# Attention scores: from half-array pairs to full-array matmuls with stacked keys

## The chip, the cores and the metric

The kernel runs on one core of a Trainium2 chip. The metric is the device time of one execution in microseconds: 1443.77 us, the median of three runs (1442.9 to 1447.32).

## The reference

Multi-head attention with two mixes over the heads, followed by two MLPs. Inputs are q, k, v of shape (4, 12, 448, 64); the rest is

```
scores = 1/sqrt(64) * q @ k^T                       # per head
scores = einsum('bhij,hg->bgij', scores, w_pre)     # mix over the 12 heads
attn   = softmax(scores)
attn   = einsum('bhij,hg->bgij', attn, w_post)
x      = (attn @ v)  as 1792 tokens x 768
x      = (s * relu(x @ w_in)**2 + b) @ w_out        # 768 -> 2048 -> 768
h      = x @ w_in2;  out = (h * cos(h)) @ w_out2
```

All of it is float32. The kernel splits the operands of the scores, the first mix and the MLPs into a high part of type float32r and the rest, and adds up three products, high x high, high x rest and rest x high; the mix after the softmax and the product with v are plain float32.

## The kernel before

The attention works on 16 blocks, four per batch, of 120, 110, 110 and 110 query rows. Per block and pair of heads (six groups g), `scores` makes two tiles of rows x 448 in PSUM, ScalarE or VectorE copies each to SBUF (L362, L364), and a DMA on SP's queue stores it into the block's tile m, in which the partition is row and head together (10 rows x 12 heads = 120 partitions): these are the DMAs `m<-s`, or `m<-at` for block 0. Then follow 12 or 11 tiles of 120 x 448 per block, 180 in all. Each is split (L417 or L419 high part, L422 rest), mixed on TensorE (L427 to L429, three passes against a 120 x 120 weight), its maximum taken (L438, VectorE), exponentiated (L445, ScalarE), and mixed a second time with the transposing matmul L467, whose weight w (L458) carries the reciprocal of the sums. `vps` (L502) multiplies with v and `x<-xo` stores the result. The MLPs follow (L747, L810, L838); their first steps overlap the last tiles.

The operands of a score come as follows. `keys(b, g, p)` loads two heads with two DMAs into the two 64-wide halves of a raw tile, so that four transposes (L289) give a PSUM tile whose partitions 0 to 63 are one head and 64 to 127 the other. One ScalarE instruction writes the high part of both heads (L294), one VectorE instruction the rest (L296). `queries(n, g, p)` does the same for six heads of a block with one DMA: three transposes (L318), two evictions (L323, L325), two groups per block. `prod` in `scores` then makes six matmuls with K = 64: with `tile_position=(64 * z, 0)` the two heads of a group use the two halves of the array's rows side by side, three times, for the three products.

The order of the work on every engine is written by a planner (`Plan`). Each step has a position `pos`, a cost and what it waits for; `run` plays the program with these costs, gives an engine that comes free the step of lowest position among those that are ready, and emits the instructions in that order. The engines then work through their queues in order. Buffers are rings: a step that takes a buffer is not placed before the one that used it last. `STEP` is the distance of two tiles' positions, `LEAD` the position of the first tile, `OFF` says how many steps ahead of a tile's second mix its parts are due, `W1` and `W2` say where between the tiles of the block before the scores of odd and of other blocks lie, `W3` the same of keys, `PRO` the positions of block 0. All DMAs are issued by SP, in order.

Of the kernel before, what the change touches and what calls it, by code (L numbers as in the profile page):

```python
# [10 lines left out]
F32 = mybir.dt.float32  # L11
F32R = mybir.dt.float32r
I32 = mybir.dt.int32
U32 = mybir.dt.uint32
AF = mybir.ActivationFunctionType
ALU = mybir.AluOpType
# [169 lines left out]
    return c  # L186


STEP = 2484.5
LEAD = 15618.0  # L190


def attention(pl, tc, q, k, v, w_pre, w_post, cst, x, mid, left, right, psl, psr):

    nc = tc.nc
    B, H, S, D = q.shape
# [12 lines left out]
    k_p = pool(right, "a_k", side="right")  # L209
# [11 lines left out]
    def dma(pos, out, in_, nbytes, after=(), take=(), use=(), behind=()):  # L221
        return pl.add(pos, "sp", 515.0 if not use else 700.0, lambda: nc.sync.dma_start(out=out(), in_=in_()), after, take, use, nbytes=nbytes, behind=behind)
# [36 lines left out]
    kh, k_done = {}, {}  # L259
# [10 lines left out]
    def keys(b, g, p):  # L270
        hk = kh[b, g] = pl.hold(f"k{g}")
        hr = scratch[0] if b == 0 else pl.hold("rk")
        raw = lambda: piece(0, g * KW, KW)[:CH].rearrange("p (z w) -> p z w", w=2 * D) if b == 0 else hr.tile

        def load(h):
            if b and h == 0:
                hr.tile = rk_p.tile([CH, 4, 2 * D], F32, tag="rk", name="rk")
            return raw()[:, :, h * D:(h + 1) * D]
        d = []
        for h in range(2):  # L280
            d.append(dma(p - 6000, lambda h=h: load(h), lambda h=h: k[b, 2 * g + h].rearrange("(p z) d -> p z d", z=4), CH * KW * 2,
                         take=[hr] if b and h == 0 else [], behind=d if h else m_done[0][-1:] if b else [s_open]))
        bank, ring, tag = (ps_s, "ps", "s") if b else (ps_a, "pa", "a") if g % 2 else (ps_p, "pp", "p")
        hp = pl.hold(ring)

        def trans():
            hp.tile = bank.tile([128, 512], F32, tag=tag, name="tk")[:, :S]
            for z in range(4):
                nc.tensor.transpose(hp.tile[:, z * CH:(z + 1) * CH], raw()[:, z], ident[:CH, :CH])  # L289
        a = pl.add(p, "pe", 440.0, trans, d + [d_id], take=[hp, hk], use=[hr])  # L290

        def hi():
            hk.tile = k_p.tile([128, 2, S], F32R, tag=f"ks{g}", name="ks")
            nc.scalar.activation(out=hk.tile[:, 0], in_=hp.tile, func=AF.Copy)  # L294
        a = pl.add(p + 500, "act", 430.0, hi, [a])
        k_done[b, g] = [pl.add(p + 1000, "dve", 540.0, lambda: nc.vector.tensor_tensor(  # L296
            out=hk.tile[:, 1], in0=hp.tile, in1=hk.tile[:, 0].bitcast(F32), op=ALU.subtract), [a], use=[hp])]


    qh, q_done = {}, {}  # L300
# [1 line left out]
    def queries(n, g, p):  # L302
        b, (i0, rows) = n // 4, BLOCKS[n % 4]
        hr, hp = pl.hold("rq") if n else scratch[0], pl.hold("ps")
        hq = qh[n, g] = pl.hold("q")
        raw = lambda: (hr.tile if n else piece(0, 6 * KW + g * 6 * D, 6 * D))[:rows].rearrange("p (z d) -> p z d", d=2 * D)

        def load():
            if n:
                hr.tile = rq_p.tile([128, 6 * D], F32, tag="rq", name="qn")  # L310
            return raw().rearrange("p z (a d) -> p (z a) d", d=D)
        d = dma(p - 8000 if n else p - 5500, load, lambda: q[b, 6 * g:6 * g + 6, i0:i0 + rows, :].rearrange("h i d -> i h d"), rows * 3072,
                take=[hr] if n else [], behind=m_done[0][5:6] if n else [s_open])

        def trans():
            hp.tile = ps_s.tile([128, 512], F32, tag="s", name="tq")[:, :3 * rows].rearrange("p (z w) -> p z w", z=3)
            for z in range(3):
                nc.tensor.transpose(hp.tile[:, z], raw()[:, z], ident[:rows, :rows])  # L318
        a = pl.add(p, "pe", 3 * rows * .87, trans, [d, d_id], take=[hp, hq], use=[hr])

        def hi():
            hq.tile = [q_p.tile([128, 3, 120], F32R, tag=t, name=t)[:, :, :rows] for t in ("qh", "ql")]
            nc.scalar.activation(out=hq.tile[0], in_=hp.tile, func=AF.Copy)  # L323
        a = pl.add(p + 600, "act", 360, hi, [a])
        q_done[n, g] = pl.add(p + 1200, "dve", 445, lambda: nc.vector.tensor_tensor(  # L325
            out=hq.tile[1], in0=hp.tile, in1=hq.tile[0].bitcast(F32), op=ALU.subtract), [a], use=[hp])


# [9 lines left out]
    def scores(n, g, p):  # L338
        b, (i0, rows) = n // 4, BLOCKS[n % 4]
        if g == 0:  # L340
            mh[n] = pl.hold("m")
        hm, hk, hq = mh[n], kh[b, g], qh[n, g // 3]
        hps = [pl.hold("ps"), pl.hold("ps")]

        def prod():
            for h in hps:
                h.tile = ps_s.tile([128, 512], F32, tag="s", name="sps")[:rows, :S]
            for y, (i, j) in enumerate(((0, 0), (0, 1), (1, 0))):
                for z in range(2):
                    part = slice(64 * z, 64 * z + 64)  # L350
                    nc.tensor.matmul(out=hps[z].tile, lhsT=hq.tile[i][part, g % 3], rhs=hk.tile[part, j], start=(y == 0), stop=(y == 2), tile_position=(64 * z, 0))  # L351
        a = pl.add(p, "pe", QK, prod, k_done[b, g] + [q_done[n, g // 3]] + m_first.get(n, []), take=hps + ([hm] if g == 0 else []), use=[hk, hq])
        m_first.setdefault(n, [a])
        for z in range(2):
            h, hp, hs = 2 * g + z, hps[z], pl.hold("s") if n else scratch[1]
# [9 lines left out]
            e = pl.add(p + 500 + 50 * z, EV, (430.0, 535.0), evac, [a], take=[hs] if n else [], use=[hp])  # L365
# [5 lines left out]
            m_done.setdefault(n, []).append(dma(p + 1000 + 50 * z, place, held, rows * S * 4, [e], use=[hs], behind=m_done.get(n, [])[:1]))  # L371

    for g in range(6):
        if g % 3 == 0:
            queries(0, g // 3, PRO[0] * g + PRO[1])
        keys(0, g, PRO[0] * g)
        scores(0, g, PRO[0] * g + PRO[2])
    for n in range(1, NBLK):
        b, kk = divmod(n, 4)
        if kk in (1, 3):  # L380
            lo, hi = pos(first[n - 1]) + (W1[0] if n > 1 else 0) * STEP, pos(first[n - 1]) + W1[1] * STEP
        else:
            lo, hi = pos(first[n - 1]) + W2[0] * STEP, pos(first[n]) - W2[1] * STEP
        w = (hi - lo) / 6
        ps = [lo + w * (g + .5) for g in range(6)]
        if kk == 0:
            for g in range(6):
                keys(b, g, pos(first[n - 2]) + (W3[0] + g * W3[1]) * STEP)
        for g in range(6):
            if g % 3 == 0:  # L390
                queries(n, g // 3, ps[g] - w - 2500)
            scores(n, g, ps[g])

    for b in range(B):
# [10 lines left out]
    for s in range(NTL):  # L405
# [510 lines left out]
```

## Time and profile before

| | |
|---|---|
| median of three runs | 1443.77 us |
| profiled execution | 1444.58 us, span 1442.8 us |
| TensorE matmul | 1399.9 us busy, 97% of the span, 8316 instructions |
| VectorE | 1189.4 us, 82% |
| ScalarE | 725.8 us, 50% |
| GpSimd | 619.2 us, 43% |
| DMA | 123.67 MB, mean 86 GB/s |
| chain that ended last | PE 87%, DMA 5%, DVE 4%, ACT 2% |

A profile is one execution; busy times are sums over its instructions. PE is TensorE, PEld its weight loads, DVE VectorE, ACT ScalarE, POOL GpSimd, SP the engine that issues the DMAs. L351 is line 351 of the kernel. Two float32r matmuls that follow each other overlap in the profile, because the end of a matmul is modelled: what one costs is read from start to start, not from its duration. A float32 matmul appears as two instructions.

### The profile page before, as it was taken

Reading aid. Unit: us, or ns where it says so; the run is one execution under the profiler, and the core shown is the slowest. Engines: PE = TensorE matmul, PEld = TensorE weight load, DVE = VectorE, ACT = ScalarE, POOL = GpSimd, SP = SyncE. Lnnn points to the kernel's source line nnn. Section 1 sums busy time; section 2 is a strip of 40 time slices with the busy share of each in tenths; the row PEclk is TensorE's granted clock in tenths of the full one; section 3 lists DMA queues with packets and bytes.
Section 4 is the critical chain, followed back from the end, with each engine's and each line's share of the span. In section 5 each row is a group of like instructions: output and inputs, shape, how many; then the busy total and the mean of one; then the engine's idle time right before and its main releaser. Section 6 shows DMA issues by size and latency. Waiting matters only on the chain.

```text
span 1442.8 us, 23086 instructions
## 1 busy us (share of the span) xinstructions
PE 1399.9 (97%) x8316; PEld 1191.8 (83%) x8316; DVE 1189.4 (82%) x2198; ACT 725.8 (50%) x1523; POOL 619.2 (43%) x553
## 2 busy tenths in 40 slices
PE   6899999999999899999999999999999999999998
PEld 4777777777777678888888888889899899998998
DVE  4777698778788888998877877898998899999975
ACT  3665575565655755333232322347654545454542
POOL 1554464444544644434242332324544454544431
PEclk8999999999999999999999999999999999999999
DMA  6545354363454242222211212111211111211103
GB/s 170 125 129 137 98 154 127 120 148 106 121 145 153 98 148 77 66 62 71 67 44 44 68 43 66 44 44 45 66 56 44 56 56 54 62 50 55 56 33 121
DMA packets 137116, 123.67 MB, mean 86 GB/s; under 512 B 71499, under 2 KB 124715, under 8 KB 137003
## 3 DMA queue, kind: packets, MB, share of 16 engines
q1 hardware_dynamic: 137003, 122.20, 29.5%
q8 instruction: 66, 1.08, 0.3%
q14 instruction: 47, 0.39, 0.1%
HBM read 72.46 MB, written 11.01 MB: 58 GB/s over the span
## 4 chain that ended last, share of the span: by engine, by line
PE 87%; DMA 5%; DVE 4%; ACT 2%; POOL 1%; issue 1%; SPq 0%; DVEq 0%; POOLq 0%; ACTq 0%
PE h L747 30%; PE o L838 16%; PE o L810 15%; PE a L467 8%; PE sps L351 4%; PE vps L502 4%; PE p L427 3%; PE p L429 2%; DMA m<-s 2%; PE p L428 2%; DMA qn<-in_q_dram 2%; PE tk L289 1%; DVE at L481 1%; DVE w L458 1%; PE tq L318 0%
## 5 line engine op out<-in xcount | busy, mean ns | idle before, releaser
L695 POOL TENSOR_TENSOR cm<-ca,wh 128x384 f32<-128x384 f32 x128 | 159.8, 1251 | 387.7 <-ACT wh L689 387.7
L422 POOL TENSOR_TENSOR m<-m,mh 120x448 fp32r<-120x448 f32 x180 | 207.7, 1159 | 173.7 <-ACT mh L417 166.6
L747 PE MATMUL h<-m,wh 128*128 128x512 f32 x672 | 215.8, 391 | 0.0
L747 PE MATMUL h<-x,wh 128*128 128x256 f32 (+1 forms) x768 | 189.9, 338 | 1.5 <-DVE x L723 1.5
L467 PEld LDWEIGHTS a<-w,e 120*112 120x112 f32 x1440 | 169.2, 179 | 25.0 <-issue 6.8
L467 PE MATMUL a<-w,e 120*112 120x120 f32 x1440 | 179.1, 271 | 5.1 <-DVE w L458 5.0
L697 POOL TENSOR_TENSOR wl<-cm,ce 128x384 fp32r<-128x384 f32 x128 | 145.1, 1135 | 77.3 <-DVE ce L693 73.7
L747 PE MATMUL h<-m,wl 128*128 128x512 f32 x384 | 150.3, 391 | 0.0
L747 PEld LDWEIGHTS h<-x,wh 128*128 128x128 f32 x768 | 131.7, 188 | 18.1 <-DVE x L723 2.3
L747 PEld LDWEIGHTS h<-m,wh 128*128 128x128 f32 x672 | 125.2, 188 | 25.5 <-issue 0.7
L810 PE MATMUL o<-gl,wh 128*128 128x512 f32 (+1 forms) x384 | 139.7, 364 | 0.0
L810 PE MATMUL o<-gh,wl 128*128 128x512 f32 (+1 forms) x384 | 139.6, 364 | 0.0
L810 PE MATMUL o<-gh,wh 128*128 128x512 f32 (+1 forms) x384 | 139.4, 363 | 0.0
L445 ACT ACTIVATE e<-p,st 120x448 f32<-120x448 f32 x180 | 113.6, 632 | 45.4 <-DVE st L438 39.0
L747 PE MATMUL h<-x,wl 128*128 128x512 f32 (+1 forms) x384 | 129.9, 338 | 0.0
L438 DVE TENSOR_REDUCE st<-p 120x1 f32<-120x448 f32 x180 | 110.3, 615 | 20.2 <-PE p L429 19.0
L787 POOL TENSOR_TENSOR tb<-ta,tb 128x512 f32<-128x512 f32 (+1 forms) x64 | 80.5, 1258 | 100.6 <-ACT tb L785 95.4
L417 ACT ACTIVATE mh<-m 120x448 fp32r<-120x448 f32 x131 | 75.4, 576 | 78.5 <-PE p L428 59.7
L838 PE MATMUL o<-wh,gl 128*128 128x384 f32 x448 | 114.0, 335 | 0.0
L838 PE MATMUL o<-wl,gh 128*128 128x384 f32 x448 | 113.9, 335 | 0.0
L838 PE MATMUL o<-wh,gh 128*128 128x384 f32 x448 | 113.8, 335 | 0.0
L847 DVE TENSOR_TENSOR acc<-acc,o 128x384 f32<-128x384 f32 x196 | 101.1, 544 | 14.2 <-PE o L838 13.9
(93 smaller groups left out, 3049.7 us busy)
## 6 DMA issues: line engine op xcount, KB each, us to landing
m<-s SPq DMA_DIRECT2D x144, 192.5 KB
raw<-in_moe_w_in_dram SPq DMA_DIRECT2D x64, 384.0 KB
raw<-in_moe_w_out_dram SPq DMA_DIRECT2D x64, 384.0 KB
m<-s SPq DMA_DIRECT2D x36, 210.0 KB
v<-in_v_dram SPq DMA_DIRECT2D x16, 336.0 KB
out_dram<-acc SPq DMA_DIRECT2D x14, 384.0 KB
rk<-in_k_dram SPq DMA_DIRECT2D x36, 112.0 KB
qn<-in_q_dram SPq DMA_DIRECT2D x24, 165.0 KB
```

The costliest lines, as they stand in the source:

```text
L417: nc.scalar.activation(out=hh.tile, in_=src().bitcast(F32), func=AF.Copy)
L422: a2 = pl.add(p - OFF[1] * STEP, "pool", 1110, lambda hh=hh, src=src: nc.gpsimd.tensor_tensor(out=src(), in0=src().bitcast(F32), in1=hh.ti ...
L438: nc.vector.tensor_reduce(out=hst.tile[:, 0, z:z + 1], in_=hp.tile, axis=AX, op=ALU.max, negate=True)
L445: nc.scalar.activation(out=he.tile, in_=hp.tile, func=AF.Exp, bias=hst.tile[:, 0, z:z + 1], accum_out=hst.tile[:, 1, z:z + 1])
L467: nc.tensor.matmul(out=ha.tile[:, c * L:(c + 1) * L], lhsT=he.tile[:, c * CH:(c + 1) * CH], rhs=hw2.tile[:, z], start=True, stop=True)
L695: a = pl.add(p0 + 6 * dp, "pool", 1050, lambda hm=hm, ha=ha, flat=flat: nc.gpsimd.tensor_tensor(out=hm.tile, in0=ha.tile.bitcast(F32), in1 ...
L697: got.append(pl.add(p0 + 7 * dp, "pool", 1050, lambda hm=hm, he=he, flat=flat: nc.gpsimd.tensor_tensor(out=flat(1), in0=hm.tile, in1=he.ti ...
L747: nc.tensor.matmul(out=hp.tile, lhsT=w, rhs=cols(z_, j, k)[:, 0], start=(k == 0 and y == 0), stop=(k == KD - 1 and y == 2))
L787: a = pl.add(p + 7 * dp, "pool", n * 2.4 + 100, lambda h1=h1, h2=h2: nc.gpsimd.tensor_tensor(out=h2.tile, in0=h1.tile, in1=h2.tile, op=ALU ...
L810: nc.tensor.matmul(out=hp.tile, lhsT=w, rhs=x, start=(c == 0 and y == 0), stop=(c == 1 and y == 2))
L838: nc.tensor.matmul(out=hp[e].tile, lhsT=x, rhs=w[:, e * HD:(e + 1) * HD], start=(c == 0 and y == 0), stop=(c == 1 and y == 2))
L847: got.append(pl.add(p, "dve", 470, lambda e=e, hp=hp, view=view: nc.vector.tensor_tensor(out=view(), in0=view(), in1=hp[e].tile, op=ALU.ad ...
```

## The change

Keys are stacked: tile `ks[:, z]` holds the high part of head z on that head's own 64 partitions and its rest on the other 64. Each key group has four evictions for that, two of ScalarE (high, in place) and two of VectorE (rest, to the other half of the partitions). Queries are doubled: each head's query is loaded twice, side by side, so that a transpose of 128 columns gives the same query on both halves of the partitions; a group is four heads now, three groups per block, with two DMAs each. A score of one head is then two matmuls over all 128 partitions: the high query against both parts of the key, and the rest of the query against both parts. (The product rest x rest is added with it.) Scores become steps of one head each instead of two. Costs and positions of the planner are set anew.

```diff
-STEP = 2484.5
-LEAD = 15618.0
+STEP = 2427.2
+LEAD = 16044.2
@@ keys
-        def hi():
-            hk.tile = k_p.tile([128, 2, S], F32R, tag=f"ks{g}", name="ks")
-            nc.scalar.activation(out=hk.tile[:, 0], in_=hp.tile, func=AF.Copy)
-        a = pl.add(p + 500, "act", 430.0, hi, [a])
-        k_done[b, g] = [pl.add(p + 1000, "dve", 540.0, lambda: nc.vector.tensor_tensor(
-            out=hk.tile[:, 1], in0=hp.tile, in1=hk.tile[:, 0].bitcast(F32), op=ALU.subtract), [a], use=[hp])]
+        def half(z):
+            return slice(64 * z, 64 * z + 64)
+
+        def hi(z):
+            if z == 0:
+                hk.tile = k_p.tile([128, 2, S], F32R, tag=f"ks{g}", name="ks")
+            nc.scalar.activation(out=hk.tile[half(z), z], in_=hp.tile[half(z)], func=AF.Copy)
+        k_done[b, g] = []
+        for z in range(2):
+            e = pl.add(p + 500 + 100 * z, "act", 430.0, lambda z=z: hi(z), [a])
+            k_done[b, g].append(pl.add(p + 1000 + 100 * z, "dve", 540.0, lambda z=z: nc.vector.tensor_tensor(
+                out=hk.tile[half(1 - z), z], in0=hp.tile[half(z)], in1=hk.tile[half(z), z].bitcast(F32), op=ALU.subtract), [e], use=[hp]))
@@ queries
-        d = dma(p - 8000 if n else p - 5500, load, lambda: q[b, 6 * g:6 * g + 6, i0:i0 + rows, :].rearrange("h i d -> i h d"), rows * 3072,
-                take=[hr] if n else [], behind=m_done[0][5:6] if n else [s_open])
+        d = []
+        for i in range(2):
+            d.append(dma(p - 8000 if n else p - 5500, lambda i=i: load(i), lambda: q[b, 4 * g:4 * g + 4, i0:i0 + rows, :].rearrange("h i d -> i h d"), rows * 2048,
+                         take=[hr] if n and i == 0 else [], behind=d if i else m_done[0][5:6] if n else [s_open]))
...
-            for z in range(3):
-                nc.tensor.transpose(hp.tile[:, z], raw()[:, z], ident[:rows, :rows])
-        a = pl.add(p, "pe", 3 * rows * .87, trans, [d, d_id], take=[hp, hq], use=[hr])
+            for z in range(4):
+                nc.tensor.transpose(hp.tile[:, z], raw()[:, z].rearrange("p a d -> p (a d)"), ident[:rows, :rows])
+        a = pl.add(p, "pe", 4 * rows * .87, trans, d + [d_id], take=[hp, hq], use=[hr])
@@ scores
-            for y, (i, j) in enumerate(((0, 0), (0, 1), (1, 0))):
-                for z in range(2):
-                    part = slice(64 * z, 64 * z + 64)
-                    nc.tensor.matmul(out=hps[z].tile, lhsT=hq.tile[i][part, g % 3], rhs=hk.tile[part, j], start=(y == 0), stop=(y == 2), tile_position=(64 * z, 0))
-        a = pl.add(p, "pe", QK, prod, k_done[b, g] + [q_done[n, g // 3]] + m_first.get(n, []), take=hps + ([hm] if g == 0 else []), use=[hk, hq])
+            def prod(z=z, h=h, hp=hp):
+                hp.tile = ps_s.tile([128, 512], F32, tag="s", name="sps")[:rows, :S]
+                for y in range(2):
+                    nc.tensor.matmul(out=hp.tile, lhsT=hq.tile[y][:, h % 4], rhs=hk.tile[:, z], start=(y == 0), stop=(y == 1))
+            a = pl.add(p + QZ * z, "pe", 410.0, prod, k_done[b, g] + [q_done[n, g // 2]] + m_first.get(n, []), take=[hp] + ([] if h else [hm]), use=[hk, hq])
@@ second mix
-            a = pl.add(p_, "pe", 888, mixt, [aw], take=[ha], use=[he, hw2])
+            a = pl.add(p_, "pe", 820, mixt, [aw], take=[ha], use=[he, hw2])
@@ constants
-PRO = (743.4, 36.7, 1160.0, -399.1)
-VW = (7, 11)
+PRO = (776.2, 851.5, 1160.0)
+VW = (7, 13)
-OFF = (4.214, 4.208, 3.018, 2.518, 2.539, 1.245)
-AVP = (2.713, 2909.7)
+OFF = (4.214, 4.426, 3.27, 2.518, 2.539, 1.825)
+AVP = (2.733, 2696.6)
-QK = 720.0
-W1 = (-1.242, 4.472)
-W2 = (-1.352, 6.158)
-W3 = (2.491, 1.454)
+QZ = 999.947
+W1 = (-1.242, 4.431)
+W2 = (-1.044, 7.344)
+W3 = (3.273, 1.708)
-TOK = ((-16000.0, 3982.1), (-1854.7, -4326.0), (6127.9, -940.2), (9977.5, 1672.7))
-WT0 = (-11360.2, -6972.4, 3371.0, 1338.6)
-TAIL = 14010.5
+TOK = ((-16472.3, 4086.8), (-2471.6, -3159.8), (5875.1, -2048.3), (9977.5, 1672.7))
+WT0 = (-11360.2, -7991.8, 3765.5, -865.2)
+TAIL = 11267.2
```

## Rows read from the trace of the kernel before

**Rows 1.** Windows; columns: window, length, busy time of each engine, clock, DMA share, GB/s.
```profile
30.00:60.00 30.00, 26.15 (x148) 21.21 (x149) 19.44 (x41) 17.64 (x44) 18.27 (x19) 0.83 0.73 158
60.00:470.00 410.00, 396.08 (x3045) 312.68 (x3043) 325.10 (x669) 255.07 (x612) 205.54 (x201) 1.00 0.47 130
470.00:520.00 50.00, 43.89 (x300) 35.59 (x300) 40.70 (x83) 33.35 (x75) 29.40 (x21) 1.00 0.38 118
520.00:1442.80 922.80, 917.20 (x4741) 811.09 (x4739) 793.53 (x1390) 408.71 (x775) 365.19 (x309) 1.00 0.19 59
```

**Rows 2.** Timeline of TensorE around scores; columns: start, length, then the instruction.
```profile
60.36 0.66 PE L351 MATMUL sps<-ks,qh 64*110 64x448 f32 x4
...
204.19 0.67 PE L351 MATMUL sps<-ks,qh 64*110 64x448 f32 x4
...
205.61 0.46 PE L427 MATMUL p<-mh,wp_h 120*120 120x448 f32 x1
205.92 0.36 PE L428 MATMUL p<-mh,wp_l 120*120 120x448 f32 x1
206.12 0.36 PE L429 MATMUL p<-m,wp_h 120*120 120x448 f32 x1
206.32 0.98 PE L467 MATMUL a<-w,e 120*112 120x120 f32 x8
...
208.99 0.36 PE L429 MATMUL p<-m,wp_h 120*120 120x448 f32 x1
209.28 0.67 PE L351 MATMUL sps<-ks,qh 64*110 64x448 f32 x4
...
210.07 0.46 PE L427 MATMUL p<-mh,wp_h 120*120 120x448 f32 x1
210.38 0.36 PE L428 MATMUL p<-mh,wp_l 120*120 120x448 f32 x1
...
456.52 0.66 PE L351 MATMUL sps<-ks,qh 64*110 64x448 f32 x4
```

**Rows 3.** Timeline of TensorE around three query transposes.
```profile
298.75 0.45 PE L318 MATMUL tq<-ident,qn 110*128 110x110 f32 x3
298.96 0.44 PE L427 MATMUL p<-mh,wp_h 120*120 120x448 f32 x1
299.24 0.37 PE L428 MATMUL p<-mh,wp_l 120*120 120x448 f32 x1
```

**Rows 4.** Groups by line: the key evictions; count, busy us, mean ns, idle before.
```profile
L296 DVE TENSOR_TENSOR ks<-tk,ks 128x448 fp32r<-128x448 f32 x24 | 14.8, 620 | 10.9 <-ACT ks L294 10.8
...
L294 ACT ACTIVATE ks<-tk 128x448 fp32r<-128x448 f32 x24 | 12.9, 542 | 15.3 <-PE tk L289 15.3
```

**Rows 5.** Windows at five changes of block; not all five are shown.
```profile
78.00:85.00 7.00, 5.50 (x39) 4.07 (x39) 4.88 (x13) 4.99 (x13) 3.39 (x4) 1.00 0.46 116
137.00:146.00 9.00, 5.52 (x38) 4.20 (x38) 5.70 (x14) 4.75 (x13) 3.10 (x4) 1.00 0.58 149
...
375.00:384.00 9.00, 5.92 (x45) 4.60 (x43) 5.88 (x14) 5.02 (x13) 3.50 (x5) 1.00 0.53 146
sum 33.00, PE 22.71 PEld 16.86 DVE 21.35 ACT 18.36 POOL 16.26; mean PE 4.54 PEld 3.37 DVE 4.27 ACT 3.67 POOL 3.25
```

**Rows 6.** Timelines of SP, ScalarE and TensorE at one change of block.
```profile
366.71 9.56 SPq L222 DMA_DIRECT2D m<-s  x8
...
380.95 0.58 ACT L417 ACTIVATE mh<-m 120x448 fp32r<-120x448 f32 x1 [2.21 <-DMA m<-s]
...
381.73 0.47 PE L427 MATMUL p<-mh,wp_h 120*120 120x448 f32 x1 [1.36 <-POOL mh L419]
```

**Rows 7.** Timelines of SP and ScalarE in the first 30 us.
```profile
3.31 3.90 SPq L222 DMA_DIRECT2D at<-in_k_dram  x6
...
29.35 0.58 ACT L417 ACTIVATE mh<-m 120x448 fp32r<-120x448 f32 x1 [2.92 <-DMA m<-s]
```

**Rows 8.** The page's DMA queue: packets, MB, share of 16 engines' span.
```profile
q1 hardware_dynamic: 137003, 122.20, 29.5%
```

More of the change, by code (lines that the diff above doesn't have):

```diff
@@ L305, in queries @@
         hq = qh[n, g] = pl.hold("q")
[L306 to L311, printed above, removed]
-        d = dma(p - 8000 if n else p - 5500, load, lambda: q[b, 6 * g:6 * g + 6, i0:i0 + rows, :].rearrange("h i d -> i h d"), rows * 3072,
-                take=[hr] if n else [], behind=m_done[0][5:6] if n else [s_open])
+        raw = lambda: (hr.tile if n else piece(0, 6 * KW + g * 8 * D, 8 * D))[:rows].rearrange("p (z a d) -> p z a d", a=2, d=D)
@@ L315, in trans, with load @@
+        def load(a):
+            if n and a == 0:
+                hr.tile = rq_p.tile([128, 8 * D], F32, tag="rq", name="qn")
+            return raw()[:, :, a]
+        d = []
+        for i in range(2):
+            d.append(dma(p - 8000 if n else p - 5500, lambda i=i: load(i), lambda: q[b, 4 * g:4 * g + 4, i0:i0 + rows, :].rearrange("h i d -> i h d"), rows * 2048,
+                         take=[hr] if n and i == 0 else [], behind=d if i else m_done[0][5:6] if n else [s_open]))
         def trans():
-            hp.tile = ps_s.tile([128, 512], F32, tag="s", name="tq")[:, :3 * rows].rearrange("p (z w) -> p z w", z=3)
@@ L317, in trans @@
-            for z in range(3):
-                nc.tensor.transpose(hp.tile[:, z], raw()[:, z], ident[:rows, :rows])
-        a = pl.add(p, "pe", 3 * rows * .87, trans, [d, d_id], take=[hp, hq], use=[hr])
+            hp.tile = ps_s.tile([128, 512], F32, tag="s", name="tq")[:, :4 * rows].rearrange("p (z w) -> p z w", z=4)
+            for z in range(4):
+                nc.tensor.transpose(hp.tile[:, z], raw()[:, z].rearrange("p a d -> p (a d)"), ident[:rows, :rows])
+        a = pl.add(p, "pe", 4 * rows * .87, trans, d + [d_id], take=[hp, hq], use=[hr])
@@ L321, in hi @@
         def hi():
-            hq.tile = [q_p.tile([128, 3, 120], F32R, tag=t, name=t)[:, :, :rows] for t in ("qh", "ql")]
+            hq.tile = [q_p.tile([128, 4, 120], F32R, tag=t, name=t)[:, :, :rows] for t in ("qh", "ql")]
             nc.scalar.activation(out=hq.tile[0], in_=hp.tile, func=AF.Copy)
-        a = pl.add(p + 600, "act", 360, hi, [a])
-        q_done[n, g] = pl.add(p + 1200, "dve", 445, lambda: nc.vector.tensor_tensor(
+        a = pl.add(p + 600, "act", 460, hi, [a])
+        q_done[n, g] = pl.add(p + 1200, "dve", 530, lambda: nc.vector.tensor_tensor(
@@ L341, in scores @@
             mh[n] = pl.hold("m")
[L342 to L347, printed above, removed]
-            for y, (i, j) in enumerate(((0, 0), (0, 1), (1, 0))):
-                for z in range(2):
-                    part = slice(64 * z, 64 * z + 64)
-                    nc.tensor.matmul(out=hps[z].tile, lhsT=hq.tile[i][part, g % 3], rhs=hk.tile[part, j], start=(y == 0), stop=(y == 2), tile_position=(64 * z, 0))
-        a = pl.add(p, "pe", QK, prod, k_done[b, g] + [q_done[n, g // 3]] + m_first.get(n, []), take=hps + ([hm] if g == 0 else []), use=[hk, hq])
-        m_first.setdefault(n, [a])
-        for z in range(2):
-            h, hp, hs = 2 * g + z, hps[z], pl.hold("s") if n else scratch[1]
+        hm, hk, hq = mh[n], kh[b, g], qh[n, g // 2]
+        for z in range(2):
+            h, hp, hs = 2 * g + z, pl.hold("ps"), pl.hold("s") if n else scratch[1]
+            def prod(z=z, h=h, hp=hp):
[3 more added lines that the diff above has]
+            a = pl.add(p + QZ * z, "pe", 410.0, prod, k_done[b, g] + [q_done[n, g // 2]] + m_first.get(n, []), take=[hp] + ([] if h else [hm]), use=[hk, hq])
+            m_first.setdefault(n, [a])
             held = lambda h=h, hs=hs: hs.tile if n else piece(1, h * S, S)[:rows]
@@ L364, in evac @@
                     nc.vector.tensor_copy(out=held(), in_=hp.tile)
-            e = pl.add(p + 500 + 50 * z, EV, (430.0, 535.0), evac, [a], take=[hs] if n else [], use=[hp])
+            e = pl.add(p + QZ * z + 500, EV, (430.0, 535.0), evac, [a], take=[hs] if n else [], use=[hp])
             def place(h=h):
@@ L370, in place @@
                 return hm.tile.bitcast(F32).rearrange("(r h) t j -> r h t j", h=H)[:, h, :rows // R]
-            m_done.setdefault(n, []).append(dma(p + 1000 + 50 * z, place, held, rows * S * 4, [e], use=[hs], behind=m_done.get(n, [])[:1]))
+            m_done.setdefault(n, []).append(dma(p + QZ * z + 1000, place, held, rows * S * 4, [e], use=[hs], behind=m_done.get(n, [])[:1]))
     for g in range(6):
-        if g % 3 == 0:
-            queries(0, g // 3, PRO[0] * g + PRO[1])
+        if g % 2 == 0:
+            queries(0, g // 2, PRO[0] * g + PRO[1])
         keys(0, g, PRO[0] * g)
@@ L389, in attention @@
         for g in range(6):
-            if g % 3 == 0:
-                queries(n, g // 3, ps[g] - w - 2500)
+            if g % 2 == 0:
+                queries(n, g // 2, ps[g] - w - 2500)
             scores(n, g, ps[g])
```

## The prediction

> **What bounds the kernel now.** I read the windows first, then TensorE's timeline around the scores, then the places where TensorE stands still, and asked at each who ended the wait. The windows show an engine that is nearly always occupied: from 60 to 470 us TensorE is busy for 396.08 of 410 us at full clock, and after 520 us, in the MLP that the diff leaves alone, for 917.20 of 922.80 us [rows 1]. So a microsecond of TensorE work taken out of the attention stage is a microsecond of the whole, and one added is lost. The idle time is the second account. Of the 13.9 us between 60 and 470 us, five changes of block hold 33.00 - 22.71 = 10.3 us [rows 5]; 3.85 us lie between 30 and 60 us and 6.1 us between 470 and 520 us [rows 1]. VectorE (325.10 of 410 us) and ScalarE (255.07) have room.
>
> **Scores.** A group of two heads is six matmuls now, three passes of two half-array matmuls side by side. Two groups in a row take from 204.19 to 205.61, 1.42 us; one alone takes from 209.28 to 210.07, 0.79 us [rows 2]. The second of a pair so costs 0.63 us, three passes of 0.21. A group alone costs more than its 0.79: from the L429 before it (208.99) to the L428 behind it (210.38) are 1.39 us, and the two full-array passes that would remain are 0.205 us each (205.92 to 206.12 to 206.32, less the rounding) [rows 2], so it costs 1.39 - 0.41 = 0.98 us. Some 0.35 us are thus paid for going from full-array work to half-array work and back. Between 60 and 470 us the timeline has 84 of the 96 groups: 74 alone, the first at 60.36 and the last at 456.52 [rows 2], and five pairs.
>
> The change makes four full-array matmuls of 448 columns of a group. Their nearest row is the full-array float32r pass just named: 4 x 0.205 = 0.82 us, and no change of array shape around it, as L428 and L429 have none. That is 74 x (0.82 - 0.98) = -11.8 us for the groups alone and 5 x (1.64 - 1.61) = +0.15 us for the pairs, -11.7 us in all. Ends: if all the 0.35 us stayed, a group alone would cost 1.17 and the term were 74 x 0.19 + 5 x 0.38 = +16 us; nothing in the rows makes it better than -13 us. I take -11.7, since the row is the same kind of instruction.
>
> **A rule against it.** The Trainium skill, TensorEngine Tiling (Array Packing), section Theoretical Speedup, promises up to twice the speed for a contraction of 64 or less, and by that rule undoing the packing should lose. The pair in [rows 2] agrees as to the passes (0.63 us against 0.82), and the rule leaves out the 0.35 us. By the rule alone the score term would be 84 x 0.19 = +16 us; its time is among the rivals.
>
> **Query transposes.** Each head's query is now loaded twice and transposed by itself: 12 transposes per block for 6, 96 more, 90 of them after the first block. Three of them stand between a mix's L429 and the next: from 298.75 to the L428 at 299.24 are 0.49 us, of which one 0.205 us pass is L427's, so a transpose costs 0.095 us [rows 3]. 90 x 0.095 = +8.6 us; those of the first block fall into its waits. TensorE's work therefore changes by only -11.7 + 8.6 = -3.1 us.
>
> **Evictions.** A key group's two evictions become four on half the partitions with the same 448 columns. No row shows one of 64 partitions, nor one that writes the other half; a cost that halves with the partitions would make them free, and I take the full price of L294 and L296, 0.54 and 0.62 us [rows 4]. 24 key evictions and 16 query evictions more on either engine, and 32 query evictions a third wider (at most a quarter of the same prices), give ScalarE 40 x 0.54 + 32 x 0.14 = 26 us and VectorE 40 x 0.62 + 32 x 0.155 = 30 us over the attention stage. VectorE goes from 79 to about 86% of 60 to 470 us. TensorE's work hides that; where the cover is thin, the row maxima and weights come late. The idle time outside the changes of block is 13.9 - 10.3 = 3.6 us; from none to a doubling of it is 0 to +3.6 us, while better positions could take some away. I take +1 us.
>
> **Query loads and the start.** 32 loads become 96, each on SP's queue, and the bytes double: 5.5 MB more. Queue q1 has 137003 packets, 122.20 MB and 29.5% of the engines' span, 426 us [rows 8]; 5.5 MB are 19 us of that by bytes and the 21504 packets of 256 B 67 us by packets, spread over 460 us where the DMA share is 0.47 [rows 1]: hidden, unless a store stands behind them. At the start SP itself is the queue: six loads take 3.90 us there, 0.65 each, and the first mix waits until 29.35 us for block 0's last store to land [rows 7]. Four more loads for block 0 and a second copy for block 1 are 5 x 0.65 = 3.3 us ahead of that store. TensorE can use a part for block 1's scores. Between 0 (the loads fit into SP's waits) and 4 us I take +2.5 us.
>
> **Changes of block.** At 375 us the eight last stores of block 12 occupy SP from 366.71 to 376.27, ScalarE starts the first tile's high part at 380.95 on the landing of a store, and TensorE waits for GpSimd's, 1.36 us before L427 at 381.73 [rows 6]. All five stretches are of this kind, the first tile of an even block. The diff moves just these scores: their window ended 6.158 steps of 2484.5 ns before the block's first tile, 15.3 us, and now ends 7.344 x 2427.2 = 17.8 us before it, while the high part stays due at 10.5 and 10.2 us. The stores gain 2.8 us, more than any one wait of these stretches. The planner also gets nearer to what a group costs: it counted 720 ns where the timeline has 980 alone, and counts 820 now, so stores are less late against their places. What is late next is the chain of mix, maximum and exponential at these places (the 375 us stretch begins with it). Bounds: nothing of the 10.3 us, or all of it. I take three quarters, -7.5 us.
>
> TAIL, WT0 and TOK move the MLP's first steps by up to 3 us among work that exists; no term, since the positions set only an order.
>
> **Sum.** The profiled execution took 1444.6 us (span 1442.8), 0.8 above the median. 1444.6 - 11.7 + 8.6 + 1 + 2.5 - 7.5 = 1437.5 us, and 1436.7 set against the median: 1437.
>
> **Rivals.** (1) The changes of block keep their wait, because it is the landing of a store and the chain behind it, and an earlier place in the order doesn't make the engines faster. Then -3.1 + 1 + 2.5 remains: 1444. For it: the wait that ends at 380.95 is for a landing, not for an engine [rows 6]. Against it: the odd blocks, whose stores are placed earlier, show no such stretch.
>
> (2) Slower, by SP's queue. Per block it issues six query loads for two, 4 x 0.65 = 2.6 us, and SP works in order: a load that waits for its ring slot (two slots, three groups a block) holds the stores behind it, and those of the seven even blocks are the ones waited for. If all of it reaches the landing, 7 x 2.6 = 18 us: 1444.6 - 3.1 + 3.5 + 18 = 1463; with half, 1454. It decides where the shift exceeds the 2.8 us gained; measurably slower begins where the idle time at the changes of block grows by 4 us. For it: the eight stores take 9.56 us of SP [rows 6]. Against: loads are placed 8 us ahead, where SP also waits for evictions.
>
> (3) The change does not do what it says: the 0.35 us stay, or the pair's 0.63 us is what a group really costs; either makes the score term +16 us. 1444.6 + 16 + 8.6 + 3.5 - 7.5 = 1465. Against it is every mix, whose passes follow other full-array work at 0.205 us.
>
> (4) More is gained: all 10.3 us go, and half of the 3.85 and 6.1 us before and after [rows 1] with them: 1444.6 - 3.1 + 2.5 - 10.3 - 5 = 1429, 1428 against the median.
>
> **Chances.** Forecast 0.54, (1) 0.22, (2) 0.14, (3) 0.03, (4) 0.07. About 0.3%, 4.3 us, is what a measurement can tell from no change, so faster means under 1439.4. The forecast's own range is 1432 to 1442 (boundary term -10 to -4, start 0 to 4); 0.46 of its 0.54 lies under 1439.4, with (4) 0.53. Same: 0.08 + (1)'s 0.22 less 0.01, 0.29. Slower: 0.18. The range that leaves out half of (4) and the upper half of (2) and (3) is 1428 to 1453.
>
> **What would show it.** In the profile after: a score matmul pair at 0.41 us spacing with 0.205 us from L429 into it and out of it; 192 transposes; no 0.5 to 1.8 us hole before the first L427 of an even block; the first high part at about 32 us instead of 29.35; half-partition evictions at 0.54 and 0.62 us. The prediction is wrong if the holes at the changes of block stay as they are, if stores land later behind query loads, or if full-array passes of scores come out above 0.21 us.

## The result and the profile after

The changed kernel takes 1461.97 us (1461.33 to 1466.36), the kernel before 1443.68 us beside it: a ratio of 1.0128, interval [1.0102, 1.0154]. It is slower by 18 us, and 1437 us had been forecast. The profiled execution has a span of 1464.4 us against 1442.8. These are lines of its page (busy time and share; queue with packets, MB and share of 16 engines; TensorE's groups with the idle time before them):

```profile
span 1464.4 us, 23087 instructions
...
PE 1411.6 (96%) x8220; PEld 1228.8 (84%) x8220; DVE 1202.2 (82%) x2195; ACT 766.5 (52%) x1605; POOL 622.2 (42%) x554
...
q1 hardware_dynamic: 159371, 127.73, 31.0%
```

The bytes are as forecast, 5.5 MB more than in [rows 8]. The windows answer to [rows 1] (busy us and instruction count of PE, PEld, DVE, ACT, POOL, then granted clock, DMA share, GB/s):

```profile
30.00:60.00 30.00, 24.96 (x153) 21.78 (x152) 19.82 (x42) 18.54 (x44) 15.51 (x15) 0.84 0.83 175
60.00:470.00 410.00, 391.23 (x2845) 334.75 (x2844) 312.90 (x638) 283.63 (x670) 205.58 (x201) 0.98 0.51 133
470.00:520.00 50.00, 39.60 (x284) 32.53 (x284) 39.28 (x78) 33.61 (x77) 24.09 (x20) 0.93 0.41 133
520.00:1464.40 944.40, 938.06 (x4876) 826.48 (x4872) 815.77 (x1413) 416.79 (x790) 376.80 (x314) 1.00 0.20 61
```

Between 60 and 470 us TensorE now stands idle for 18.8 us, where it was 13.9, and between 470 and 520 us for 10.4, where it was 6.1. From 30 to 60 us the DMA share went from 0.73 to 0.83.

Three sums over TensorE's records divide the span: idle time (no matmul running), time lost to the clock (half of the busy time in stretches granted at half), and work, the rest. Before: 42.9 + 8.7 + 1391.2. After: 52.8 + 17.9 + 1393.8. So of 21.6 us, 9.9 are idle time, 9.2 clock and 2.6 work. The profiled execution is the longest of the four (1466.36 us, mean granted clock 0.984; the others took 1461.33 to 1462.18 at 0.988 or 0.989), so a part of its 9.2 us of clock is its own. By place: the first mix is 4.5 us later (34.83 against 30.29), the first mix of block 15 14.8 later, the last mix (the first mix of the last tile) 20.3 later; the MLP adds the last 1.3 us.

The single steps came out as priced. TensorE's timeline, scores in a row and then four and four query transposes behind a mix [answers to rows 2 and 3]:

```profile
206.28 0.36 PE L433 MATMUL p<-m,wp_h 120*120 120x448 f32 x1
206.49 0.92 PE L326 MATMUL tq<-ident,qn 110*128 110x110 f32 x8
207.24 1.81 PE L471 MATMUL a<-w,e 120*112 120x120 f32 x16
...
210.50 0.36 PE L357 MATMUL sps<-ks,ql 128*110 128x448 f32 x1
210.70 0.36 PE L357 MATMUL sps<-ks,qh 128*110 128x448 f32 x1
210.90 0.37 PE L357 MATMUL sps<-ks,ql 128*110 128x448 f32 x1
211.10 0.37 PE L431 MATMUL p<-mh,wp_h 120*120 120x448 f32 x1
211.31 0.36 PE L432 MATMUL p<-mh,wp_l 120*120 120x448 f32 x1
```

A score pass starts 0.20 us after the one before, and so does the mix behind it: nothing is paid between scores and mixes any more. Eight transposes take 0.75 us, 0.094 each. The groups by line and shape (count, busy us, mean ns, idle before) show the key evictions [answer to rows 4]: half the partitions cost as much as all, also where the rest goes to the other half.

```profile
L302 DVE TENSOR_TENSOR ks<-tk,ks 64x448 fp32r<-64x448 f32 x48 | 29.9, 622 | 15.4 <-ACT ks L298 14.4
...
L298 ACT ACTIVATE ks<-tk 64x448 fp32r<-64x448 f32 x48 | 25.7, 536 | 13.0 <-PE tk L289 12.7
```

At the start [answer to rows 7], SP's timeline and the first high part:

```profile
1.19 2.71 SPq L222 DMA_DIRECT2D at<-in_k_dram  x4
3.94 1.14 SPq L222 DMA_DIRECT2D at<-in_q_dram  x2
...
20.82 1.05 SPq L222 DMA_DIRECT2D qn<-in_q_dram  x2
...
23.69 4.25 SPq L222 DMA_DIRECT2D m<-at  x5
...
33.04 0.58 ACT L421 ACTIVATE mh<-m 120x448 fp32r<-120x448 f32 x1 [1.15 <-DMA qn<-in_q_dram]
```

Block 0's last stores leave SP at 27.9 us, and the first high part starts at 33.04 where it was 29.35. One hole at a change of block [answer to rows 6; block 4], on SP, TensorE, VectorE and ScalarE, and then TensorE's windows around it:

```profile
138.31 7.34 SPq L222 DMA_DIRECT2D m<-s  x6
...
140.38 0.37 PE L433 MATMUL p<-m,wp_h 120*120 120x448 f32 x1
...
142.10 0.62 DVE L368 COPY s<-sps 120x448 f32<-120x448 f32 x1 [1.70 <-DMA m<-s]
143.29 0.54 ACT L366 ACTIVATE s<-sps 120x448 f32<-120x448 f32 x1 [4.14 <-DMA m<-s]
...
143.78 1.05 PE L471 MATMUL a<-w,e 120*112 120x120 f32 x8 [3.03 <-DVE w L462]
```

```profile
140.40:143.80 3.40, 0.37 (x3) 0.05 (x1) 1.53 (x5) 0.51 (x2) 1.69 (x2) 1.00 0.59 185
143.80:145.20 1.40, 1.40 (x11) 1.36 (x12) 0.96 (x2) 1.12 (x4) 0.00 (x0) 1.00 0.52 143
145.20:148.60 3.40, 3.36 (x15) 2.78 (x14) 2.31 (x6) 2.48 (x7) 1.07 (x1) 0.50 0.55 167
```

The score copies stand in order on VectorE and ScalarE, and these two wait until a store has freed a slot; maxima, exponentials and weights stand behind them, and so TensorE waits 3.03 us for w. From 1.4 us after the hole the granted clock is 0.50 for 3.4 us, 1.2 in place of 2.4 GHz, which takes another 1.7 us. Two more waits for w end at 265.34 (2.39 us) and 386.85 (2.08 us), and one wait for ScalarE at 491.24 (3.97 us). Half-clock stretches up to 520 us add up to 44 us after, 17 of them between 22 and 39 us, and to 20.5 before.

### The profile page after: what moved, and what is told of

Read it like the earlier page. It is cut to its first block, busy times and chain, and to the rows that moved or that the text cites. A ratio compares the mean times of both kernels' runs of the same rounds, so it can differ in the third digit from the quotient of the medians.

```text
span 1464.4 us, 23087 instructions
## 1 busy us (share of the span) xinstructions
PE 1411.6 (96%) x8220; PEld 1228.8 (84%) x8220; DVE 1202.2 (82%) x2195; ACT 766.5 (52%) x1605; POOL 622.2 (42%) x554
## 4 chain that ended last, share of the span: by engine, by line
PE 85%; DMA 6%; DVE 5%; ACT 2%; POOL 1%; issue 1%; SPq 1%; DVEq 0%; POOLq 0%; ACTq 0%
PE h L751 30%; PE o L842 16%; PE o L814 15%; PE a L471 8%; PE vps L506 5%; PE sps L357 4%; DMA m<-s 2%; PE p L431 2%; PE p L433 2%; PE p L432 2%; DMA qn<-in_q_dram 1%; PE tq L326 1%; DVE st L442 1%; DMA m<-x 1%; SPq L222 1%
## 5 line engine op out<-in xcount | busy, mean ns | idle before, releaser
L471 PEld LDWEIGHTS a<-w,e 120*112 120x112 f32 x1440 | 172.8, 182 | 32.7 <-issue 13.4
L701 POOL TENSOR_TENSOR wl<-cm,ce 128x384 fp32r<-128x384 f32 x128 | 148.3, 1160 | 83.2 <-DVE ce L697 79.2
L449 ACT ACTIVATE e<-p,st 120x448 f32<-120x448 f32 x180 | 114.1, 634 | 37.0 <-DVE st L442 34.6
L675 DVE SCALAR_TENSOR_TENSOR cm<-cm,raw 128x384 f32<-128x384 f32 x128 | 95.7, 748 | 20.2 <-ACT cm L673 20.1
```

The costliest lines, as they stand in the source:

```text
L449: nc.scalar.activation(out=he.tile, in_=hp.tile, func=AF.Exp, bias=hst.tile[:, 0, z:z + 1], accum_out=hst.tile[:, 1, z:z + 1])
L675: a = pl.add(p0 + dp, "dve", 470, lambda hm=hm, high=high: nc.vector.scalar_tensor_tensor(out=hm.tile, in0=hm.tile, scalar=2.0 ** -15, in1 ...
L701: got.append(pl.add(p0 + 7 * dp, "pool", 1050, lambda hm=hm, he=he, flat=flat: nc.gpsimd.tensor_tensor(out=flat(1), in0=hm.tile, in1=he.ti ...
```

## The experiments

Each ran beside the kernel before on the same chip. The theories at the beginning: A, the new positions squeeze the scores of even blocks; B, the doubled query loads; C, the added evictions; D, the price of changing the array's shape; E, the new written order as such.

**Positions and slots of the changed kernel.** x1 puts the scores' window of even blocks back, x2 gives stores seven slots, x4 puts all positions back.

```diff
 # x1, against after
-W2 = (-1.044, 7.344)
+W2 = (-1.352, 6.158)
 # x2, against after
-N_S = 4
+N_S = 7
 # x4, against after: STEP, LEAD, PRO, VW, OFF, AVP, W1, W2, W3, TOK, WT0, TAIL of before, and
-QZ = 999.947
+QZ = 410.0
```

> The changed kernel with one constant of before: W2 = (-1.352, 6.158), so that the scores of the even blocks are spread over a longer stretch again. Theory A (packing: the scores of an even block are packed into a stretch in which their stores cannot leave, so score evictions wait for one of the four slots, stand in ScalarE's and VectorE's queues in front of the exponentials, maxima and weights, TensorE waits 2 to 3 us, and its clock is halved behind that): the holes of over 2 us at 140, 262 and 384 us go, 6 to 12 us less than the 1462 of the change, 1450 to 1456. Theory B (the doubled query loads delay the stores on SP's queue): holes stay, 1459 to 1465. Theory C (the added evictions fill ScalarE and VectorE): 1459 to 1465.

> The changed kernel with N_S = 7 in place of 4: seven SBUF slots between a score's eviction and its store; positions unchanged (the planner knows of the slots). Theory A (packing): evictions no longer wait for a slot, 6 to 12 us less, 1450 to 1456, and the idle time of VectorE and ScalarE put down to the stores' landing goes from over 10 us to near none. Theory B (query loads on SP): the stores land as late as now, the first mix of even blocks waits as long, 1458 to 1464. Theory C (evictions): no change, 1460 to 1464.

> The new scores, keys and queries with every position of before (STEP, LEAD, PRO, VW, OFF, AVP, W1, W2, W3, TOK, WT0, TAIL; 410 ns between the two heads of a group, 36.7 ns for the queries of block 0). Theory A (packing by the new positions is what costs): 1440 to 1449, near the kernel before. Theory B (query loads) and theory C (evictions), which sit in the new structure: 1455 to 1466, as the change.

x1: 1461.9 us, 1.012 [1.0091, 1.0149]; x2: 1469.9, 1.0166 [1.0134, 1.0198]; x4: 1458.4, 1.0093 [1.0064, 1.0123]. Theory A falls. These are waits between 36 and 520 us (total us, times, longest) of the changed kernel, then of x2:

```profile
ACT s L366 <- DMA m<-s: 17.6, 13, 4.1
...
PE a L471 <- DVE w L462: 14.7, 13, 3.0
...
DVE s L368 <- DMA m<-s: 11.4, 15, 1.7
```

```profile
PE a L471 <- DVE w L462: 4.3, 8, 1.2
DVE s L368 <- DMA m<-s: 3.6, 2, 2.4
```

With seven slots most of the score copies' waits and of TensorE's for w are gone, and the kernel is no faster (the intervals of x2 and of after overlap). In x1 the copies' waits sink from 29.0 to 8.9 us and the clock's loss from 17.9 to 9.7, while work and idle time grow by 3.6 and the time stays. So these holes, plain as they are in the trace, are not where the change's time can be had back. Old positions may save a little (the intervals of x4 and of after overlap); most of the loss isn't theirs.

**Parts of the change done to the kernel before.** x6 does the queries' part alone (loads, transposes, evictions, groups of four), with scores still in half arrays; x7 halves the key evictions in place; x8 takes the mix's new cost, and so a new order; x9 makes each query transpose twice and tells the planner so, which makes the order new; x10 issues each query load a second time: nothing reads the second copy, but the transposes wait for it; x5 places two groups of scores behind each other.

```diff
 # x6: queries() as after; scores keep tile_position
-lhsT=hq.tile[i][part, g % 3]
+lhsT=hq.tile[i][part, (2 * g + z) % 4]
 # x7
+nc.scalar.activation(out=hk.tile[half(z), 0], in_=hp.tile[half(z)], func=AF.Copy)
+out=hk.tile[half(z), 1], in0=hp.tile[half(z)], in1=hk.tile[half(z), 0].bitcast(F32)
 # x8
-a = pl.add(p_, "pe", 888, mixt, [aw], take=[ha], use=[he, hw2])
+a = pl.add(p_, "pe", 820, mixt, [aw], take=[ha], use=[he, hw2])
 # x9
-            for z in range(3):
+            for z in (0, 1, 2, 0, 1, 2):
-        a = pl.add(p, "pe", 3 * rows * .87, ...)
+        a = pl.add(p, "pe", 6 * rows * .87, ...)
 # x10
+        d2 = dma(..., again, lambda: q[b, 6 * g:6 * g + 6, i0:i0 + rows, :]..., rows * 3072, behind=[d])
-        a = pl.add(p, "pe", ..., trans, [d, d_id], take=[hp, hq], use=[hr])
+        a = pl.add(p, "pe", ..., trans, [d, d2, d_id], take=[hp, hq], use=[hr])
 # x5
-        ps = [lo + w * (g + .5) for g in range(6)]
+        ps = [lo + w * (g // 2 * 2 + 1) + g % 2 for g in range(6)]
```

> The kernel before with one line of positions: groups 2i and 2i+1 of a block get the same place, so that their half-array passes stand side by side and the way into and out of the half-array shape (0.35 us) is paid once for two groups. 59 stretches of scores for 85 by the order of TensorE. Theory D (the way between the array's shapes is a real cost of TensorE): 26 x 0.35 = 9 us of TensorE's work go; 1434 to 1440, less if the scores' copies then wait. If the 0.35 us are no cost of TensorE (it would have waited there anyway): 1443 to 1448. Theory E (any new order costs some us, because the positions of before fit its own steps): 1440 to 1452.

> The kernel before with the query part of the change alone: each query loaded twice, 12 transposes per block for 6, three groups per block with wider evictions; scores on half arrays and keys as before, positions of before. Transposes alone, at 0.095 us: +9 us. With the start (four more loads, 2 to 4 us): 1454 to 1458, and this part holds nearly all of the loss that x4_old_positions has against the kernel before (13 us), because the scores' gain in it would be small. If the loss sits in the key evictions or in the scores: 1444 to 1450.

> The kernel before with the key evictions alone made in halves: two of ScalarE and two of VectorE on 64 partitions each, in place, everything else as before. Theory C (added evictions fill ScalarE and VectorE): +4 to +8 us, 1448 to 1452. Otherwise within 2 us of before, 1442 to 1446. Theory E (any new order): 1440 to 1452.

> The kernel before with one number of its planner: the second mix counts 820 ns for 888, as in the change. No instruction is added or taken away, only the order is made anew. Theory E (any new order costs some us): 2 to 8 us off the kernel before, up or down. Otherwise within 2 us, 1442 to 1446.

> The kernel before with every query transpose made twice into the same place (96 more transposes, no more loads or evictions), positions of before. If TensorE's work adds up one to one at 0.095 us: +9 us, ratio 1.006. If the transposes cost more where they stand between half-array scores: +12 us, 1.008. If waits take them in: under +4 us, 1.003.

> The kernel before with every query load issued twice, the second into room that nothing reads (32 more DMAs on SP's queue, 5.5 MB more), positions of before. Theory B in its narrow form (the loads cost at the start alone): first mix 1 to 2 us later than at 30.3 us (two more loads ahead of it in block 0), time +1 to +3 us, ratio 1.001 to 1.002. Theory B in its wide form (loads delay stores in every block): +6 us or more, 1.004 and up. If queries alone (+15 us) is transposes (+9 to +12) plus this, the two must add up.

| run | us | ratio | idle + clock + work |
|---|---|---|---|
| x5 pairs | 1446.8 | 1.0007 [.9992, 1.0022] | 48.4 + 9.1 + 1385.4 |
| x6 queries | 1461.8 | 1.0101 [1.0071, 1.0132] | 46.4 + 11.4 + 1402.8 |
| x7 key halves | 1442.6 | 0.9976 [.9963, .999] | 39.8 + 7.3 + 1394.5 |
| x8 order | 1443.7 | 0.9985 [.9969, 1.0] | 41.4 + 10.8 + 1389.8 |
| x9 transposes | 1447.7 | 1.0011 [.9996, 1.0025] | 34.6 + 5.3 + 1402.3 |
| x10 loads | 1458.3 | 1.0096 [1.0071, 1.012] | 50.0 + 9.0 + 1395.5 |

x6 has nearly the whole loss, and x10 shows that the second loads alone, which nobody reads, make 14 us of it; x9 and x10 add up to x6 (0.11 and 0.96% against 1.01%). Evictions in halves, the order and the transposes cost nothing that can be told from no change. x9 and x5 are the surprise: windows of x9, then of x5, against 396.08 of before [rows 1].

```profile
60.00:470.00 410.00, 404.28 (x3127) 320.11 (x3124) 322.45 (x676) 252.87 (x601) 207.20 (x206) 1.00 0.47 130
```

```profile
60.00:470.00 410.00, 391.56 (x3060) 318.81 (x3058) 320.26 (x669) 255.03 (x614) 215.29 (x215) 1.00 0.47 131
```

11.1 us of added work on TensorE were taken in by its waits (the idle time sinks by 8.3, the clock's loss by 3.4); 5.8 us less work became waits (5.5 more idle). Both runs also have a new order; but the orders that x8 and x14 (below) write moved the time by some 2 us, which hides no 11. x8 shows the same from another side. These are the first mix of block 15 and the last mix on TensorE's timeline, in the kernel before and then in x8:

```profile
469.32 0.46 PE L427 MATMUL p<-mh,wp_h 120*120 120x448 f32 x1
...
489.84 0.44 PE L427 MATMUL p<-mh,wp_h 120*120 120x448 f32 x1
```

```profile
461.25 0.46 PE L427 MATMUL p<-mh,wp_h 120*120 120x448 f32 x1
...
489.63 0.45 PE L427 MATMUL p<-mh,wp_h 120*120 120x448 f32 x1
```

x8 is 8.1 us ahead at block 15 and 0.2 at the last mix, x14 9.5 and 2.1, x5 5.2 and 2.3: most of what was gained up to there is lost in the last block, where the MLP's first steps stand between the tiles and VectorE and ScalarE are busier than TensorE (18.3 and 17.0 against 16.1 of the 20 us from 470 to 490 in the kernel before). Which of them holds the end back no run separates. TensorE's work alone, though it is busy for 97% of the stretch, does not set the end here.

**Other ways to double.** x3 loads each query once and lets GpSimd copy it; x11 (positions of before) loads and transposes once and doubles by evictions of half the partitions, four on ScalarE and four on VectorE for six heads.

```diff
 # x3, against after
-        for i in range(2):
+        for i in range(1):
+        d = [pl.add(p - 2000, "pool", 600.0, lambda: nc.gpsimd.tensor_scalar(out=raw()[:, :, 1], in0=raw()[:, :, 0], ...), d)]
 # x11, against x4
+            nc.scalar.activation(out=hq.tile[0][half(y), z], in_=hp.tile[half(z)], func=AF.Copy)
+            nc.vector.tensor_tensor(out=hq.tile[1][half(y), z], in0=hp.tile[half(z)], in1=hq.tile[0][half(z), z].bitcast(F32), op=ALU.subtract)
```

> The changed kernel with each query loaded once and copied to its second place by GpSimd (48 copies of 110 x 256 in place of 48 of the 96 loads). Theory B (query loads): 8 to 14 us less, 1448 to 1454, and the stores of the even blocks are issued earlier. Theory A (packing): only the start gains, 1 to 3 us, 1459 to 1461, the holes at 140, 262 and 384 us stay. Theory C (evictions): the same as A, 1459 to 1462.

> Full-array scores and stacked keys as in the change, positions of before, but each query is loaded once and transposed once for two heads as before; the doubling is made by evictions that write the other half of the partitions (four of ScalarE and four of VectorE on 64 partitions per group of six heads, 128 in all for either engine in place of 48). Theory F (the scores' gain on TensorE, 8 to 10 us of work, is real and is eaten by the transposes and by loads): 12 to 18 us under x4_old_positions, 1438 to 1446, at or under the kernel before. Theory C (added evictions fill ScalarE and VectorE; some 60 us more on the two than in the change): 1450 to 1462.

x3: 1464.8, 1.0151 [1.0112, 1.0189]. It moves no more bytes than the kernel before (122.20 MB), and theory B expected 1448 to 1454: that failed. The first mix comes at 32.2 instead of 34.8 us, and by block 6 that is given back (209.9 and 209.3). GpSimd stands for 22.6 us before nine of the copies, waiting for a load, with the mixes' operands behind them; whether that took up what the loads gave back, no run separates. x11: 1486.6, 1.0279 [1.0249, 1.0309], the dearest; its groups by line:

```profile
L336 DVE TENSOR_TENSOR ql<-tq,qh 64x330 fp32r<-64x330 f32 x96 | 47.8, 498 | 11.7 <-ACT qh L333 10.1
L333 ACT ACTIVATE qh<-tq 64x330 fp32r<-64x330 f32 x96 | 42.3, 440 | 3.7 <-PE tq L324 2.0 <-DVE ql L336 0.4
```

TensorE's idle time rises to 70.3 us. x11 has fewer loads and transposes than x4, so its loss is put down to the evictions, 128 for 48 on either engine; its new order is not told apart from them. Two more evictions per key group cost nothing.

**How the loads cost.** In all of these the kernel before is the base. x12: the second load brings one head of six. x13: full second loads, but for blocks 0 and 1 alone. x16: full second loads everywhere, while the planner is told x12's bytes, so that every engine has exactly x12's order.

```diff
 # x12, against x10
-q[b, 6 * g:6 * g + 6, i0:i0 + rows, :] ... rows * 3072, behind=[d])
+q[b, 6 * g:6 * g + 1, i0:i0 + rows, :] ... rows * 512, behind=[d])
 # x13, against x10
+        d2 = [...] if n < 2 else []
 # x16, against x10
-rows * 3072, behind=[d])
+rows * 512, behind=[d])
```

> The kernel before with every query load followed by a second one, as in x10, but the second brings one head of the six (0.9 MB in all instead of 5.5 MB). Nothing reads it. Theory B1: the second loads of x10 cost through their bytes and 256-byte packets, which stand ahead of the stores and loads that the blocks wait for; then a sixth of the bytes costs a sixth, 2 us, and the time is 1444 to 1448. Theory B2: they cost through SP, where each DMA is one more issue in order and one more landing that the transposes wait for; then 32 small ones cost as much as 32 large ones, 1455 to 1460.

> The kernel before with the second loads of x10 (all six heads) for blocks 0 and 1 alone: 4 instead of 32. Theory B-start: what x10 lost was the first mix 4 us later and all that hangs on it, so these four cost nearly all: 1455 to 1458. Theory B-blocks: the loss is made block by block, and only the first mix's 4 us, or less, is left: 1446 to 1449. Theory A (the scores' packing) says nothing of this run.

> The second loads of x10, all six heads and unread, but the planner is told the bytes of x12's small ones, so that every engine has exactly the order of x12; only the bytes of 32 transfers differ. If the chip's transfers cost the time (bytes and packets ahead of stores and loads), it comes out as x10: 1455 to 1459. If the order that the planner wrote for larger transfers cost it, as x12: 1446 to 1450.

x12: 1448.4, 1.0019 [1.0006, 1.0032]; x13: 1453.3, 1.0054 [1.0034, 1.0074]; x16: 1455.9, 1.0085 [1.0069, 1.0101]. The same number of issues, in the same order, costs 3 us with a sixth of the bytes and 12 us with all of them: most of it is the bytes, or the 256-byte packets that grow with them, and not SP's issues. (x12's 3 us are issues, a sixth of the bytes and a new order together.) Windows of x12, then of x16, and the DMA engines' busy tenths in 40 slices of 0 to 60 us:

```profile
0.00:30.00 30.00, 16.85 (x87) 10.59 (x87) 10.62 (x20) 10.20 (x19) 0.20 (x4) 0.82 0.62 162
30.00:60.00 30.00, 27.24 (x164) 20.61 (x164) 23.64 (x49) 21.15 (x50) 20.15 (x18) 0.84 0.71 169
```

```profile
DMA  0269778675667763556766769767999779857200
```

```profile
0.00:30.00 30.00, 17.86 (x87) 11.19 (x87) 10.54 (x20) 10.32 (x19) 0.20 (x4) 0.87 0.70 165
30.00:60.00 30.00, 23.03 (x126) 17.10 (x127) 18.26 (x37) 16.66 (x41) 16.82 (x15) 0.78 0.83 187
```

```profile
DMA  0379999996666676235668666779767999986998
```

In x16 the engines are at nine tenths or more in thirteen slices, from 4.5 to 13.5 us without a break; in x12 in six. Its first mix comes 2.2 us after x12's (33.7 and 31.5), block 1's 5.8 us after (60.7 and 54.9), and 5.5 us are left at the last mix: the difference of the two profiles (5.7 us; the medians differ by 7.5) is made in the first 61 us. A part of it goes through the added wait of the transposes: block 0's second ones start at 15.30 us in x16 and at 13.58 in x12. x13 says the same with 4 loads of 32, which cost 8 of x10's 14 us. The Trainium skill, DMA: Bandwidth & Descriptors, section Issuing engines are not separate DMA queues, calls the time to initiate a DMA usually small beside the DMA itself; x12 and x16 agree, 3 us against 12.

**The same in the changed kernel.** Both against x4. x15 loads the queries of blocks 0 and 1 once, with GpSimd's copies. x17 tells the planner half of the loads' bytes.

```diff
 # x15
-        for i in range(2):
+        for i in range(2 if n > 1 else 1):
+        if n < 2:
+            d = [pl.add(p - 2000, "pool", 600.0, ...)]
 # x17
-rows * 2048,
+rows * 1024,
```

> The change's structure at the positions of before (x4, 1458.4), with the queries of blocks 0 and 1 loaded once and copied to the second place by GpSimd; from block 2 on both loads stay. Theory B-start: the second loads at the start cost the change what they cost the kernel before in x13, 8 us, less the GpSimd copies: 1450 to 1454. If the start's price is taken up elsewhere in the changed kernel (as in x3, whose copies run through all blocks), nothing: 1457 to 1460.

> The change's structure at the positions of before (x4, 1458.4), both query loads as they are, but the planner is told half of their bytes, so that the order is written for about the bytes that queries had before. If the order written for doubled bytes costs, 1449 to 1454; if the transfers themselves, 1457 to 1461.

x15: 1456.1, 1.0083 [1.0052, 1.0113], not told from x4. Its first mix is 2.4 us earlier than x4's (31.7 and 34.1), at block 4 0.3 us of that are left. x17: 1465.6, 1.0157 [1.0138, 1.0175]: the order alone moved x4 by 7 us for the worse. Both expectations that the loads' price can be had back this way failed; no run of the changed kernel, x3 included, shows it.

**What cost nothing, together.** x14 is x7 with x8's cost.

> The kernel before with the two parts of the change that cost nothing alone: keys evicted in halves in place (x7, ratio 0.9976) and the mix at 820 ns in the written order (x8, 0.9985). If both gains were real and add up, 0.996, 1438 us; if they are what any new order of the queues moves, 0.996 to 1.002, 1438 to 1447.

1442.5, 0.9985 [.9973, .9996]. The gains don't add up; x14 and x7 are the only versions whose interval lies below 1, by 0.15 and 0.24%, less than the 0.3% that this kernel's measurement can tell.

## Why the prediction was wrong

- **The premise failed first**: that a microsecond of TensorE's work is one of the whole. Work taken out turned into waits (x5), work added filled waits (x9). Even 8.1 us of lead at block 15 were gone at the last mix (x8). So neither the -11.7 nor the +8.6 us could be entered in the sum one to one, whatever their sizes.
- **Scores, -11.7.** The passes are right, 0.20 us, and the change of shape is gone. The Trainium skill, TensorEngine Tiling (Array Packing), section Key Properties, says that a change of tiling mode drains TensorE; these lines against [rows 2] agree. By sums, work falls from 1402.8 (x6) to 1395.4 (x4) or 1393.8 (after), 7 to 9 us, so a little was over-counted; the sum is no clean price, since it also counts the modelled end of the matmul before each hole, 0.36 us where a pass in a row is 0.20 (x11, with the transposes of before and 94 holes for 42, has 1395.1 against 1391.2). In time the change that the title names is worth next to nothing: x4, which differs from x6 by full-array scores of one head a step, stacked keys and some numbers of the planner, has a ratio of 1.0093 against 1.0101, and the intervals overlap.
- **Transposes, +8.6.** 96 transposes more are 11.1 us of work in x9, and no time that can be told from none.
- **Evictions, +1.** The price per instruction was right (622 and 536 ns), and x7 shows no cost for the keys.
- **Query loads and start, +2.5.** This is the term that was mis-sized: 12 to 14 us (x16, x10), measured in the kernel before. The prediction counted SP's issues, which with a sixth of the bytes and a new order come to 3 us (x12), and called the bytes hidden, by a DMA share of 0.47 that is the mean of 60 to 470 us. [rows 1] had 0.73 for 30 to 60 us, and there the engines fill up. The start itself came out near: the first high part at 33.04 us where about 32 was expected.
- **Changes of block, -7.5.** The wrong sign: idle time between 60 and 470 us grew by 4.9 us, and the holes moved from the first mix of a block to w, in the hole shown behind score copies that wait for slots, with half clock after it. Rival (1) said that the waits stay. The moved window and the slots don't explain the loss: x1 and x2 take most of the copies' waits away, and no time.
- **Rival (2)** had the place, SP's loads, and with 1454 to 1463 the time, at a chance of 0.14. Its mechanism, issues that hold up stores in even blocks, isn't what x12 and x16 show.

What stays open: the loads explain 12 to 14 of 18 us as measured in the kernel before; that they cost as much in the changed kernel is not shown, since x3 and x15, which take half of them away wholly or at the start, are not told from the kernels they were made from. There the delay at the start is regained (x4 is level with before at block 7's first mix, 236.1 and 236.3 us, where x10 is at 240.3) and the loss comes late: x4 is 5.3 us behind at block 15's first mix, and from there to the last mix it takes 26.1 us, as after does, for 20.5 before. x8 and x14 spend 28 us in that stretch and lose nothing in all, so it isn't a price by itself. No run separates it, and x17 shows that an order may move the time by 7 us.

## What to carry to other kernels

Before counting an engine's work one to one, double or drop some of it: a stage at 97% may still not be paced by it. Price a doubled load in the window in which it moves, by its bytes and the DMA share there, not by the mean share and not by issues alone. When a planner writes the order, compare variants in the same written order, as x12 and x16 do; otherwise the order's own microseconds stand in the difference.

## What was not expected of the hardware

An eviction of 64 partitions took as long as one of 128 (622 and 536 ns for 448 columns, against 620 and 542), also into the other half of the partitions. A hole of 3.03 us on TensorE was followed, 1.4 us after work began again, by 3.4 us at a granted clock of 0.50, which took another 1.7 us. And 4.6 MB more in unread loads, some 4% of the bytes, cost 7 to 10 us with the order unchanged (x16 against x12), while the DMA engines stood at nine tenths or more in thirteen of the 40 slices of the first 60 us, for six.
